# A spectral layer and a mixture of experts on one core: two row groups per gating step, early row fetches tied to their own scatters, zeros in the row memory, a fixed prologue, and a new written order

## The chip, the cores and the metric

The program runs on one NeuronCore of a Trainium2 chip. The metric is the device time of one execution in microseconds. Engines are named as the profile names them: PE is the matmul engine and PEld its weight loads, DVE the vector engine, ACT the scalar engine, POOL the GpSimd engine, and SP the engine that only issues DMAs (SPq, ACTq and POOLq are the instruction queues).

## The reference

The input x has 8 batches of 1856 rows of 256 values. The first half is a spectral layer, the second a mixture of 16 experts in which each row goes to exactly one.

```python
X = np.fft.rfft(x, axis=1);  Xr, Xi = X.real, X.imag
Yr = Xr @ w_r - Xi @ w_i + b_r
Yi = Xr @ w_i + Xi @ w_r + b_i
Yr, Yi = soft_threshold(Yr, 0.01), soft_threshold(Yi, 0.01)
y = np.fft.irfft(Yr + 1j * Yi, n=1856, axis=1).reshape(14848, 256)

g = argmax(y @ w_group)                 # one of 4 groups, and its softmax weight
e = argmax(y @ w_expert[g])             # one of 4 experts of that group, and its weight
out[row] = weight_g * weight_e * (relu(y @ w1[g, e]) @ w2[g, e])
```

## The kernel before

Both Fourier transforms are matmuls with constant matrices. The batches go through in four pairs. For a pair, `first_a` (L342) and `turn_a` (L372) do the first transform stage over eight chunks of x. Fifteen frequency blocks follow: `f_mm` (L668) is the second stage, `f_high`, `f_im`, `f_low`, `f_sum`, `s_high` and `s_low` split its result into high and low parts, `m_both` and `m_each` (L723) multiply by the mixing weights, and `m_re`, `m_relu` and `m_min` (L733, L745, L752, L754) add the bias and apply the threshold. When all fifteen blocks are done, `b_mm` and `b_turn` (L771, L780), then `p_mm` and `p_out` (L790, L801, L803) transform back. The rows of a pair then lie in `vs[pr]`, one half of the tile `vv`; pairs 0 and 2 use the first half, pairs 1 and 3 the second. The second half also serves as the landing place of pair 1's x at the start.

A pair's rows come in eight groups. For each group `p_turn` (L812) turns the rows, `p_copies` (L816) copies them to the tile `yt`, `g_mm` (L831) computes the gate logits and `g_turn` (L841) turns them back. After four groups `route_g` chooses the experts of half a pair, in 32 small steps, most of them on DVE; the 31st (L280) writes `sloti`, the row's place in the list of its expert. Then each of the 16 row sets of that half is sent by one indirect DMA on POOL (`scatter`, L293) to `xs_d`, the lists in HBM: eight halves, 128 scatters. `FLY = (2, 2, 2, 4)` says how many scatters of a pair may be under way: a scatter waits until the one `FLY` before it has landed. Before that, `clear_steps` fills the first 1152 places of each list with zeros, 16 DMAs of 1170 KB from the ACT queue (L436).

For experts 0 to 3 the first 512 rows of each list are computed early, as eight jobs of 256 rows, in between the work of the spectral half: `e_fetch` (L472 and L477, DMAs on SP), `e_ids`, `e_turn` (L481), `e_high` (L892), `e_low` (L896), then `up_mm` (L907) and `down_mm` (L928, L929) with their followers, and `down_out`, a store by an indirect DMA on POOL (L578). Rows 0 to 255 of a list come from pairs 0 and 1, that is from scatters 1 to 64, rows 256 to 511 from pair 2, scatters 65 to 96. The early jobs alternate: expert 0 first half, expert 0 second half, expert 1 first half, and so on. The tiles of the early jobs lie in pools that are opened when the last `m_min` of the last pair is in the list, in the memory of the pools `cf` and `wf` that close there.

The order of PE, ACT and DVE in this first part is written out by hand: the string `ORDER` has one letter per step, and a letter calls the next step of its kind. POOL is not bound to the list. SP's queue is in list order too, but not the prologue's. After the list the remaining rows of all experts are computed by a loop over `JOBS` (L520, L592, L593 and their followers) until the end.

The letters used in the text: e `f_mm`, f `f_high`, g `f_im`, h `f_low`, i `f_sum`, t `s_high`, u `s_low`, j `m_bias`, k `m_both`, q `m_re`, p `m_each`, o `m_min`, c `a_mm`, r `b_mm`, s `b_turn`, y the copy to `yt`, G `g_mm`, H `g_turn`, R a step of routing, S a scatter, Z a clear, F `e_fetch`, T `e_turn`, X `e_high`, Y `e_low`, U `up_mm`, A and B its followers, I `e_ids`, D `down_mm`, K an early store, l a load on SP.

Of the kernel before, what the change touches and what calls it, by code (L numbers as in the profile page):

```python
# [10 lines left out]
F32 = mybir.dt.float32  # L11
# [10 lines left out]
K1 = 15  # L22
# [43 lines left out]
ejefgfhitgeukhijqeptukmoqfgmhicotupjmkfoqmoghepijtefguhkmimqootcjpukdqmfZgmoehiptojfZguemkhcqmoiotjpfZukgdqehi  # L66
mmoptojfZugcmmdkhqoeitopujkmfZgomqheitpclojufZgdmkehoqmitojpfZgukmmedqhplitfZgouojmmchocioktjeqpumfZgddokmqhci
otpjumedfZogmkqehitojpukmoqefZmogpjhitemmukofZogjhrqpitsumekmsfZrgohioqstjusepfZkqgmohripmfZssmotoeghriusjekts
mocjcqdupfZkdcqmgvdompcwlohjmifmtducexdgkohyqcivdopwGHlmcvemfjtoguwhiotkxquypjefkmdomgchvoiqtduGpjwxmkmfgqhyix
ltpoHGeoHjmumkoyfgoqhivtGpHRjeuwRRfkRmglqRxeomhioRpvtjfyRukmRRRqRgehmRRiptGRRomoRHfomujRvegRokhwRqxiRjtuwRpRfk  # L70
gRmxqRmhioopytjRuGmmyRHkqefoopgRhiemtjumGfkooRqgrhjiptuekRHfmegsRsmohiRrSqotussjpkmfmqvogowjpxheityukrqfGmgRom
phsHesmfoRitjouRgrkhieqstRmepsSmSoucRRjSSRvkwRdSRfcgSRxqRhmpyivdSocRtofgGuhRwcSmdljRRiHRdRRkqxomyecSStcRpRRoRd
dRufGljvghcwkHiRxmmqoRpeSytdojRRfScgRmvuhoRmwkqeiRtdlupojfGHSvRkqxmmwRRogpeyoShmSxiGtomvSufghjHRRkiqoteRRRSSRy
pjSuRkvRRmfqGoghwSpmioRteRjuRkRSSHfmxqoSpRghmRoyeRiRSwGtSmjvfwSSRRRRRuSgHkRqhiRxRtmoxRSoRpSyjeuRRkGRfqghimomyp
mmeoRHotoGHuRRfRjSghitrkujeqsRRspRmfkgomRqhrRopssmeSjRfiotRgumrhRitkSReqloRpSusRjfkesmgRRmoqhriotRSjRpuRmSskfW
gqoSmshReiWpmSfvSRgoSvRhtSeuRimjRokqVRSwxowRStuSjpRRkySGmRqmSxRHVfRpgRheyoiWoSSvvWGStVmSSfgjuwokShqwxipmoyeHjm
GtfxgSSmoyHhuekioRGWqHjRRRvwRtpRmRfvRRgRxuwRRShRkWRomqieotSpjukRmfmRRReRgyqVWhRipRSSfoRoxvgRhGmtjmiuRtkuSRRyoq
pRSoRSSWRjRRRVHRwSSekSmfxvghieotmqGoVwHyjpmVVfSxughoGimyotSHGuSSSHljRkkRRSqRRqpRSRSRRRmpmomSRRmoSRoRoRRRRRRFrR
ssRTXRrRYRsSURARRsRUSRRBrUASSABsUSsrSIABBsSDDESsvvSSwwSDWWxJRVvwDSxyGyESvxHGyVSwvHwvxwGWHyvGSWSwSxSHRRSRxyGRRR
# [1314 lines left out]
```

## Time and profile before

| | |
|---|---|
| median of 3 runs | 1055.45 us (1054.57 to 1057.11) |
| the profiled execution | 1054.6 us, span 1052.8 us |
| PE busy | 1016.0 us, 97% of the span |
| DVE, ACT, POOL busy | 704.4, 549.6, 255.1 us |
| mean granted PE clock | 0.993 of 2.4 GHz |
| first part (the written order) | about 0 to 466 us |

The span runs from the first to the last instruction. PE is busy almost throughout, so what counts is where it is not, and where its clock is granted at half. An engine that is idle elsewhere costs nothing unless PE or the chain of rows waits for it. A row of the timeline gives start, duration, engine, line, operation and, in brackets, the idle time before it with what ended it.

### The profile page before, as it was taken

How to read it: one execution, taken by the hardware profiler on the slowest of the kernel's cores; microseconds unless marked ns; L12 is line 12 of the kernel's file. 1: busy time of each engine (PE TensorE's matmuls, PEld its weight loads, DVE VectorE, ACT ScalarE, POOL GpSimd, SP SyncE). 2: the span in 40 equal slices, each digit the busy share in tenths (PEclk: the TensorE clock that was granted, in tenths of full speed). 3: DMA queues.
4: the chain of work that ended last, by engine and by line, in shares of the span. 5: the costliest groups of instructions: out<-in, count | busy, mean ns of one | idle time of the engine just before them, and what ended most of it. 6: DMA issues, size and time to landing. Idle time of an engine off the chain costs nothing.

```text
span 1052.8 us, 20013 instructions
## 1 busy us (share of the span) xinstructions
PE 1016.0 (97%) x7078; PEld 857.9 (81%) x7078; DVE 704.4 (67%) x1764; ACT 549.6 (52%) x1428; POOL 255.1 (24%) x262
## 2 busy tenths in 40 slices
PE   7999999999996999999999999999999999999996
PEld 4886787677874678998899999988889899999995
DVE  6889678988987477647677656475465566566551
ACT  2664685575873464434554535455354455455442
POOL 1000003245355517641121211212211121212111
PEclk9999999999998999999999999999999999999998
DMA  9776401421132156565343232431431431432100
GB/s 379 289 308 239 162 1 38 158 87 69 51 103 81 65 140 185 171 204 148 113 138 112 59 109 53 145 115 49 136 111 51 138 107 52 146 113 63 33 26 25
DMA packets 110065, 125.62 MB, mean 119 GB/s; under 512 B 86250, under 2 KB 86923, under 8 KB 105098
## 3 DMA queue, kind: packets, MB, share of 16 engines
q1 hardware_dynamic: 91386, 74.31, 24.1%
q0 software_dynamic: 11888, 30.67, 7.8%
q10 hardware_dynamic: 6688, 19.34, 4.7%
q8 instruction: 57, 0.93, 0.4%
q14 instruction: 46, 0.38, 0.1%
HBM read 74.32 MB, written 51.75 MB: 120 GB/s over the span
## 4 chain that ended last, share of the span: by engine, by line
PE 79%; issue 6%; DVE 5%; DMA 4%; ACT 3%; POOL 2%; SPq 1%; POOLq 0%; ACTq 0%; DVEq 0%
PE ph L520 26%; PE py L592 16%; PE pw L723 11%; PE py L593 8%; PE pg L668 4%; PE ph L907 3%; DMA xs_d<-v,sloti 2%; PE bank L771 2%; PE bank L342 2%; PE bank L790 2%; PE bank L812 1%; PE py L611 1%; POOL xs_d L293 1%; PE pg L831 1%; PE pg L928 1%
## 5 line engine op out<-in xcount | busy, mean ns | idle before, releaser
L592 PE MATMUL py<-big,hh 128*128 128x512 f32 (+2 forms) x792 | 275.9, 393 | 0.1
L520 PE MATMUL ph<-xth,big 128*128 128x384 f32 (+14 forms) x1024 | 274.3, 346 | 1.6 <-DVE hl L528 0.8
L578 POOL DMA_INDIRECT out_dram<-yo,si x120 | 122.3, 1019 | 484.8 <-DVE si L315 234.0
L528 DVE SCALAR_TENSOR_TENSOR hl<-ph,hh 128x256 fp32r<-128x256 f32 x472 | 157.5, 372 | 98.4 <-ACT hh L524 71.6
L593 PE MATMUL py<-big,hl 128*128 128x256 f32 (+2 forms) x792 | 221.0, 279 | 0.0
L524 ACT ACTIVATE hh<-ph 128x256 fp32r<-128x256 f32 x472 | 140.2, 345 | 113.3 <-PE ph L520 112.6
L520 PEld LDWEIGHTS ph<-xth,big 128*128 128x128 f32 x1024 | 185.4, 188 | 13.6 <-ACT xth L506 1.9
L293 POOL DMA_INDIRECT xs_d<-v,sloti x128 | 126.2, 986 | 284.0 <-DVE big L754 147.8
L520 PE MATMUL ph<-xtl,big 128*128 128x384 f32 (+14 forms) x512 | 176.8, 345 | 1.2 <-DVE xtl L507 1.2
L592 PEld LDWEIGHTS py<-big,hh 128*128 128x128 f32 (+2 forms) x792 | 147.4, 186 | 34.6 <-issue 1.2
L593 PEld LDWEIGHTS py<-big,hl 128*128 128x128 f32 (+2 forms) x792 | 148.0, 187 | 0.3
L600 DVE SCALAR_TENSOR_TENSOR yo<-py,si,yo 128x256 f32<-128x256 f32 (+2 forms) x99 | 47.7, 482 | 108.9 <-ACT yo L599 108.9
L599 ACT ACTIVATE yo<-py,si 128x256 f32<-128x256 f32 (+2 forms) x99 | 46.8, 473 | 131.4 <-PE py L593 121.4
L520 PEld LDWEIGHTS ph<-xtl,big 128*128 128x128 f32 x512 | 96.3, 188 | 7.0 <-DVE xtl L507 2.3
L723 PE MATMUL pw<-wh,xh 128*128 128x256 f32 x360 | 81.3, 308 | 1.6 <-DVE pw L733 1.1
L745 ACT ACTIVATE th<-pw,CF 128x256 f32<-128x256 f32 x120 | 61.1, 526 | 36.8 <-PE pw L723 23.5
L723 PEld LDWEIGHTS pw<-wh,xh 128*128 128x128 f32 x360 | 54.3, 189 | 29.0 <-DVE pw L733 9.4
L723 PE MATMUL pw<-wh,xl 128*128 128x256 f32 x360 | 71.4, 280 | 0.9 <-DVE xl L707 0.9
L723 PE MATMUL pw<-wl,xh 128*128 128x256 f32 x360 | 71.0, 279 | 0.0
L668 PEld LDWEIGHTS pg<-CF,big 128*128 128x128 f32 x480 | 58.4, 191 | 12.6 <-issue 3.1
L668 PE MATMUL pg<-CF,big 128*128 128x128 f32 x480 | 64.6, 278 | 4.2 <-DVE xs L698 2.1
L723 PEld LDWEIGHTS pw<-wh,xl 128*128 128x128 f32 x360 | 54.9, 189 | 1.1 <-DVE xl L707 1.1
(187 smaller groups left out, 1557.4 us busy)
## 6 DMA issues: line engine op xcount, KB each, us to landing
xt<-in_w_dram SPq DMA_DIRECT2D x22, 1024.0 KB, 6.1
xs_d<-zero ACTq DMA_DIRECT2D x16, 1170.0 KB, 5.0
whole<-in_w_dram SPq DMA_DIRECT2D x16, 1024.0 KB, 8.1
xt<-in_x_dram SPq DMA_DIRECT2D x8, 1024.0 KB, 5.4
xg<-xs_d SPq DMA_DIRECT2D x48, 96.0 KB, 2.3
big<-in_x_dram SPq DMA_DIRECT2D x8, 512.0 KB, 4.9
v<-in_x_dram SPq DMA_DIRECT2D x4, 1024.0 KB, 14.1
xg<-xs_d SPq DMA_DIRECT2D x24, 128.0 KB, 3.2
```

The lines of the kernel that those rows point to most:

```text
L293: ins = nc.gpsimd.indirect_dma_start(out=xs_d, out_offset=bass.IndirectOffsetOnAxis(ap=sl_, axis=0), in_=row, in_offset=None, bounds_check ...
L520: nc.tensor.matmul(o[:, :w], lhsT=a_[:, ch, fs], rhs=b_[:, ch, 0:w], start=k == 0, stop=k == 5)
L524: nc.scalar.activation(out=hh[:, f, :m], in_=ov, func=AF.Relu)
L528: nc.vector.scalar_tensor_tensor(out=hl[:, f, :m], in0=ov, scalar=0.0, in1=hh[:, f, :m].bitcast(F32), op0=ALU.max, op1=ALU.subtract)
L578: ins = nc.gpsimd.indirect_dma_start(out=out, out_offset=bass.IndirectOffsetOnAxis(ap=ids.si[0:m, t:t + 1], axis=0), in_=ysb, in_offset=No ...
L592: nc.tensor.matmul(o, lhsT=hh[:, f, ts], rhs=w2b[:, :, f, :], start=f == 0, stop=f == 7, skip_group_check=True)
L593: nc.tensor.matmul(o[:, 0:D], lhsT=hl[:, f, ts], rhs=w2h[:, f, :], start=False, stop=f == 7, skip_group_check=True)
L599: nc.scalar.activation(out=ysb, in_=o[:, D:], func=AF.Copy, scale=gate_w)
L600: nc.vector.scalar_tensor_tensor(out=ysb, in0=o[:, 0:D], scalar=gate_w, in1=ysb, op0=ALU.mult, op1=ALU.add)
L668: nc.tensor.matmul(f_view(pr, k)[:, ch, :, bt], lhsT=zys[pr][:, k, bt, ch * 128:(ch + 1) * 128], rhs=T_v[:, k, :], start=True, stop=True)
L723: nc.tensor.matmul(y[:, half * D:(half + 1) * D], lhsT=a_[:, ch, t], rhs=w_[:, t, ch], start=False, stop=True, skip_group_check=True)
L745: nc.scalar.activation(out=units["t", pr, k][:, ri], in_=psum["m", pr, k][:, ri * D:(ri + 1) * D], func=AF.Relu, bias=nlam, scale=sg_col(0 ...
```

## The change

- `g_mm` and `g_turn` take two row groups per step. The matmuls of two groups (16 of 128 columns in both cases) go to one PSUM tile, and one transpose of 256 columns replaces two of 128. `yt` has two buffers in place of one.
- An early fetch no longer depends on scatters after the 64th (first half) or 96th (second half); it waits for the last `FLY` scatters up to that one. The pools of the early jobs are opened with waits tile by tile, and a tile of 512 bytes is put ahead of the fetched rows.
- `zero` is no tile of its own; it is the first three rows of `vs[0]`, which `b_turn` of pair 0 overwrites.
- The prologue (loads, first transform stage, weights) is in a written order on PE, ACT, DVE and SP. The mixing weights `wri` are loaded behind the second chunk of x; their sums and differences are made on POOL. The last chunk of x is loaded, multiplied and turned in two halves. The constants come in three pieces; `K` is still behind all of them and ahead of pair 1's x.
- `f_low` and `f_sum` may come in either order.
- The string `ORDER` is another one. Counting letters: the first `e_fetch` stands behind 72 scatters (76 before) and is followed at once by its `e_turn` (before: five steps later). The 16 clears stand at places 1 to 245 (72 to 340 before); the first `b_turn` at 287 (275 before). The slot step of pair 1's second half stands behind 54 `m_re` (52 before); the last one, of pair 3, behind 21 `up_mm` and 17 `down_mm` (22 and 17 before), with 5 early stores between it and the last scatter (3 before).

The beginning of the list, and the stretch from the last `m_min` of pair 3 to the slot step of pair 2's second half, before and after:

```
before  ejefgfhitgeukhijqeptukmoqfgmhicotupjmkfoqmoghepijtefguhkmimqootcjpukdqmfZ
after   eZjfgZieftheuhgkijqetugiZpmofkqmcZohtpujkmgqfoihmetpgoZudejkmifocmtqgopjh
before  oRRRRRRFrRssRTXRrRYRsSURARRsRUSRR
after   oFTSrSSRXRRRYRsURURSIAsSlBRARrURARRssrRR
```

The diff, without the string and cut to its core:

```diff
+    one, three = CF1 - (K1 - 1) * 128, CF1 - (K1 - 3) * 128
+    ms.enter_context(tc.manual_schedule(engines=engines))
+    queue.enter_context(tc.manual_schedule(engines={mybir.EngineType.SP}))
+    for c in range(8):
+        if c == 2:
+            nc.sync.dma_start(out=wraw[:, 0:2].rearrange("p a c e -> p (a c e)"), in_=wri)
+        if c == 7:
+            nc.sync.dma_start(out=CF[:, 0:one], in_=cst[:, 0:one])
+            for h in (0, 512):
+                nc.sync.dma_start(out=flat[0][:, c, h:h + 512], in_=flat[1][:, c, h:h + 512])
+        else:
+            nc.sync.dma_start(out=flat[0][:, c], in_=flat[1][:, c])
+    nc.sync.dma_start(out=bias.rearrange("p a e -> p (a e)"), in_=bri)
+    nc.sync.dma_start(out=CF[:, one:three], in_=cst[:, one:three])
+    nc.sync.dma_start(out=craw, in_=cst[:, CF1:CI0])
+    nc.sync.dma_start(out=CF[:, three:], in_=cst[:, three:CF1])
+    nc.sync.dma_start(out=K, in_=cst[:, CK0:CK1])
+    for c in range(0, 8, 2):
+        nc.sync.dma_start(out=xbig[1][:, c:c + 2], in_=x_v[1, :, c:c + 2])
...
+    def last_half(h):
+        o = bank()
+        x = flat[0][:, 7, 512 * h:512 * h + 512]
+        for rows in range(2):
+            for cols in range(2):
+                nc.tensor.matmul(o[64 * cols:64 * cols + 64, 512 * rows:512 * rows + 256], lhsT=cA[64 * rows:64 * rows + 64, 0:64],
+                                 rhs=x[64 * rows:64 * rows + 64, 256 * cols:256 * cols + 256], start=True, stop=True)
...
+    nc.scalar.copy(out=wh[:, 2], in_=w_r)
+    nc.gpsimd.tensor_tensor(out=dif, in0=w_i, in1=w_r, op=ALU.subtract)
+    nc.scalar.copy(out=wh[:, 0], in_=dif)
+    nc.gpsimd.tensor_tensor(out=tot, in0=w_i, in1=w_r, op=ALU.add)
+    nc.scalar.copy(out=whs, in_=tot)
+    nc.scalar.activation(out=wh[:, 1], in_=tot, func=AF.Copy, scale=-1.0)
...
-    zero = cf.tile([128, 3, RW], F32, name="zero")
+    zero = vv[:, 0, 0:3]
...
-        yts[pr, u] = wi.tile([128, 2, 4, 128], F32, name="yt", bufs=1)
+        yts[pr, u] = wi.tile([128, 2, 4, 128], F32, name="yt", bufs=2)
...
-    @steps_of(pairs, u8)
+    @steps_of(pairs, range(0, 8, 2))
     def g_mm(pr, u):
+        o = psum["g", pr, u][:, 0:256].rearrange("p (h v z) -> p v h z", h=2, v=2)
+        for v in range(2):
+            yt = yts.pop((pr, u + v)).rearrange("p c (h x) t -> p c h x t", h=2)
...
         for ins in reads:
             tc.add_to_no_dep_group("early rows", ins.ins)
+            for k in range(64 + 32 * j, len(sent)):
+                tc.declare_no_dep(ins.ins, group=f"row{k + 1}", reason="later rows go to slots behind those of the early jobs")
+            for k in range(64 + 32 * j - FLY[1 + j], 64 + 32 * j):
+                tc.add_manual_dep(ins.ins, sent[k], landed, reason="the early job's rows have landed")
...
-                early["mp"] = ph.enter_context(tc.tile_pool(name="mp", bufs=1))
+                early["mp"] = ph.enter_context(tc.tile_pool(name="mp", bufs=1, reuse_waits="tile"))
...
+                early["mp"].tile([128, 128], F32, name="behind", bufs=1)
```

## Rows read from the trace of the kernel before

**Rows 1.** Windows: length, busy us (and count) of PE, PEld, DVE, ACT, POOL; clock, DMA share, GB/s.

```profile
15.00:25.00 10.00, 6.07 (x50) 4.99 (x43) 7.85 (x12) 5.04 (x12) 3.77 (x3) 1.00 1.03 421
105.00:300.00 195.00, 191.39 (x1804) 146.53 (x1804) 159.47 (x388) 133.27 (x311) 57.91 (x59) 1.00 0.23 81
300.00:329.20 29.20, 24.82 (x252) 20.79 (x250) 25.66 (x73) 20.70 (x47) 14.54 (x15) 1.00 0.29 99
329.20:340.20 11.00, 6.25 (x36) 1.61 (x28) 6.13 (x14) 0.62 (x1) 6.12 (x7) 0.72 0.36 102
340.20:380.20 40.00, 36.93 (x333) 24.13 (x333) 20.10 (x42) 20.00 (x40) 17.14 (x18) 0.95 0.25 68
```

**Rows 2.** Waits of SP's queue, 280 to 460 us: total us, times, longest.

```profile
SPq L472 <- DMA xs_d<-v,sloti: 75.8, 8, 36.9
SPq L472 <- DVE big L754: 24.2, 1, 24.2
```

**Rows 3.** Timeline around the first early fetch, 328 to 346 us.

```profile
328.68 0.47 DVE L754 SCALAR_TENSOR_TENSOR big<-pw,CF,th 128x256 f32<-128x256 f32 x1
...
333.70 0.38 SPq L472 DMA_DIRECT2D xi<-xs_d  x1
...
338.01 0.71 DVE L481 STREAM_TRANSPOSE sl<-xg 128x512 f32<-128x512 f32 x1 [4.46 <-DMA xg<-xs_d]
...
344.92 0.23 DVE L280 TENSOR_SCALAR sloti<-slot,K 128x16 int32<-128x16 f32 x1
```

**Rows 4.** Timeline: scatters 49, 64, 81 and 96, the second early fetch.

```profile
283.36 0.97 POOL L293 DMA_INDIRECT xs_d<-v,sloti  x1 [10.36 <-ACT big L862]
...
306.09 0.97 POOL L293 DMA_INDIRECT xs_d<-v,sloti  x1 [0.30 <-issue]
...
345.93 0.97 POOL L293 DMA_INDIRECT xs_d<-v,sloti  x1 [7.78 <-DVE hl L917]
...
370.59 0.97 POOL L293 DMA_INDIRECT xs_d<-v,sloti  x1 [0.40 <-DMA xs_d<-v,sloti]
...
372.99 0.39 SPq L472 DMA_DIRECT2D xi<-xs_d  x1
...
380.18 0.39 PE L907 MATMUL ph<-xtl,big 128*128 128x256 f32 x1 [0.22 <-DVE xtl L896]
```

**Rows 5.** Timeline: the loop's first fetch and one of its first matmuls.

```profile
456.61 0.38 SPq L472 DMA_DIRECT2D xi<-xs_d  x1
...
466.07 0.45 PE L520 MATMUL ph<-xtl,big 128*128 128x400 f32 x1 [0.31 <-DVE xtl L507]
```

**Rows 6.** Timeline of DVE: the 54th `m_re`.

```profile
294.55 0.49 DVE L733 SCALAR_TENSOR_TENSOR pw<-pw,CF,bias 128x256 f32<-128x256 f32 x1 [0.24 <-PE pw L723]
```

**Rows 7.** Groups of instructions by line, first part: busy us, mean ns, idle before.

```profile
L831 PE MATMUL pg<-yt,wg 128*32 128x128 f32 x512 | 20.6, 279 | 4.3 <-ACT yt L816 3.1 <-DVE L L841 0.8 <-DVE xs L698 0.5
L841 DVE STREAM_TRANSPOSE L<-pg 128x128 f32<-128x128 f32 x32 | 9.8, 307 | 14.9 <-PE pg L831 14.8
```

**Rows 8.** Timeline of DVE: the first `b_turn`.

```profile
82.35 1.25 DVE L780 STREAM_TRANSPOSE v<-bank 128x1024 f32<-128x1024 f32 x1 [0.38 <-PE bank L771]
```

**Rows 9.** Timeline of the prologue, 15 to 19 us.

```profile
15.09 0.62 ACT L408 CAST wh<-xt 128x512 fp32r<-128x512 f32 x1 [12.61 <-DMA xt<-in_wri_dram]
...
15.79 1.27 POOL L409 TENSOR_TENSOR wl<-xt,wh 128x512 fp32r<-128x512 f32 x1 [14.31 <-ACT wh L408]
...
17.01 1.16 PE L668 MATMUL pg<-CF,big 128*128 128x128 f32 x8 [1.48 <-DVE big L372]
...
18.87 0.69 DVE L693 TENSOR_TENSOR xl<-pg,xh 128x512 fp32r<-128x512 f32 x1 [0.32 <-ACT xim L685]
```

**Rows 10.** DMA queues, 100 to 108 us: packets, MB, share of 16 engines' time.

```profile
q1 hardware_dynamic: 272, 1.05, 38.9%
q10 hardware_dynamic: 388, 1.18, 37.0%
```

**Rows 11.** Chain of waits: one `up_mm` at full clock (start, us, matmuls).

```profile
388.42 1.42 PE ph L907 x12
```

More of the change, by code (lines that the diff above doesn't have):

```diff
@@ L377, in drain @@
             pass
[L379 removed]
+    warm = pg.tile([128, 512], F32, name="pg")
     for _ in range(14):
[L381 removed]
+        nc.tensor.matmul(warm[:, 0:256], lhsT=ones, rhs=smask[16], start=True, stop=True)
     for _ in range(2):
@@ L387, in spectral_moe @@
+    for i in range(7):
         o = bank()
         first_a(0, i, o)
-        a_last = turn_a(0, i, o)
-    craw = wf.tile([128, 2 * D], F32, name="th")[:, 0:128]
-    wraw = xp.tile([128, 4, 2, D], F32, name="xt")
-    nc.sync.dma_start(out=wraw[:, 0:2].rearrange("p a c e -> p (a c e)"), in_=wri)
-    nc.sync.dma_start(out=craw, in_=cst[:, CF1:CI0])
-    bias = cf.tile([128, 2, D], F32, name="bias")
-    nc.sync.dma_start(out=bias.rearrange("p a e -> p (a e)"), in_=bri)
-    nc.sync.dma_start(out=CF[:, first:], in_=cst[:, first:CF1])
@@ L411, in spectral_moe @@
-    mix_parts(2, 0)
-    nc.scalar.copy(out=sl, in_=craw)
-    nc.vector.tensor_tensor(out=bias[:, 0], in0=bias[:, 0], in1=bias[:, 1], op=ALU.subtract)
-    behind.close()
-    nc.vector.memset(nlam, -2 * LAM)
+        turn_a(0, i, o)
+        if i == 1:
+            for _ in range(8):
+                nc.tensor.matmul(warm[:, 0:256], lhsT=ones, rhs=smask[16], start=True, stop=True)
+    for h in range(2):
+        last_half(h)
     T_v = CF[:, CF1 - K1 * 128:CF1].rearrange("p (k m) -> p k m", m=128)
-    late = ExitStack()
@@ L427, in spectral_moe @@
     nc.sync.dma_start(out=wgp, in_=wgate)
-    late.close()
-    zero = cf.tile([128, 3, RW], F32, name="zero")
+    zero = vv[:, 0, 0:3]
     nc.gpsimd.memset(zero, 0.0)
+    cf.tile([128, 16], F32, name="behind")
     def clear_steps():
@@ L621, in spectral_moe @@
     jobs = EJOBS
-    engines = {mybir.EngineType.PE, mybir.EngineType.Activation, mybir.EngineType.DVE}
     sgo = _OFF["SG"][0]
@@ L685, in f_im, with f_read @@
         nc.scalar.copy(out=xi, in_=f_part(pr, k)[:, :, 1])
-        if pr == k == 0:
-            mix_parts(0, 2)
-            mix_parts(1, 3)
+        if (pr, k) == (0, 0):
+            nc.vector.tensor_tensor(out=bias[:, 0], in0=bias[:, 0], in1=bias[:, 1], op=ALU.subtract)
+        if (pr, k) == (0, 1):
+            nc.scalar.copy(out=sl, in_=craw)
+    read = set()
+    def f_read(pr, k):
+        if (pr, k) in read:
+            del psum["f", pr, k]
+        read.add((pr, k))
     @steps_of(pairs, k15)
```

112 lines of the change are left out of this document (50 added, 62 removed).

## The prediction

> **What bounds the kernel now.** I read the windows first. PE is the engine that counts, and the change reaches only the first part. PE stands idle there for 3.9 us between 15 and 25, for 3.6 us between 105 and 300, and for 12.2 us between 300 and 380 (4.4, 4.8 and 3.1) [rows 1]. In the worst piece, 329.2 to 340.2, the clock is also granted at 0.72 on average, part of it at the lower of the two levels.
>
> The waits of SP say why. A fetch of early rows (L472) waits for scatters eight times, 75.8 us in all, and once 24.2 us for the last `m_min` (L754) [rows 2]. The timeline shows the first: the last `m_min` starts at 328.68, the fetch is issued at 333.70, DVE stands 4.46 us before `e_turn` until the rows are there at 338.01, and behind `e_turn` DVE holds back the routing and PE [rows 3]. Then a second chain sets the pace. The slot step of pair 2's second half (344.92) releases sixteen scatters on POOL, 345.93 to 370.59, 1.64 us each; the fetch for the second early job goes at 372.99, and PE starts on it at 380.18 [rows 3, 4]. That is 35.3 us from slot step to matmul, 9.6 of them behind the last scatter's start. At the end of the first part the same happens once more: behind the last scatters the loop's first fetch goes at 456.61, and a matmul at 466.07 waits for the rows' low part [rows 5].
>
> **The change, part by part.** All times are of the profiled execution: span 1052.8 us, 1054.6 us in all, 0.85 below the median of the three runs; differences are carried over to that median.
>
> *The first early fetch.* It needs scatter 64. In the list before, 76 scatters stand ahead of it and it waits for all of them. Now it waits for two that started by 306.09 [rows 4], and, with memory released tile by tile and 512 bytes put ahead, probably for the last second-stage matmul in place of the last `m_min`. Then the rows lie ready and `e_turn` starts right behind the last `m_min`. Between that and the slot step DVE has about the same work: four `b_turn`, `e_turn` and `e_low` in both, 14 routing steps for 17, and an id step (two operations) and one low half more. So the 4.46 us of waiting go; 0.5 us I keep back for waits that it covered: -4.0 us. Bounds: 0, if the fetch stays late; -5.5, if the slow clock behind it goes too (about 3 us of 128x256 matmuls at half speed cost up to 1.5).
>
> *What is late next: POOL.* The scatters of pair 2 cannot go faster than two at a time. In the list after, the slot step of pair 1's second half stands behind 54 `m_re`, which puts it near 294.55 [rows 6], where the first of its scatters started at 283.36 before [rows 4]. POOL then has 48 scatters in a row. Spacing: 1.52 us for scatters 49 to 64, 1.64 for 81 to 96 [rows 4]; 47 spacings at 1.5 are 70.5 us. With the next item's 1.5 us the first starts near 293.9 and the last at 364.4, while the path over pair 2's own slot step gives 370.59 - 1.5 - 4.0 = 365.1. The two meet; I add 1.0 us for their interference. Bounds: 0 at 1.45 us a scatter, +6 at 1.64.
>
> *Two groups a step, two `yt` buffers.* The matmuls are the same 16 per pair of groups. DVE saves a transpose in two: 32 of 307 ns [rows 7] become 16 of 256 columns; from 307 ns for 128 columns and 1.25 us for 1024 [rows 8] one takes about 440, so 2.8 us less on an engine that is 82% busy in 105 to 300 [rows 1]. PE waited 3.1 us for `yt` in all [rows 7]. Part of the 3.6 us of idle time goes: I take -1.5 for this and the new list up to pair 3, with -3.6 (all) and +3.6 (as much new) as ends. What pays is the logits: a pair of groups is turned back only when both are done, which is one reason why the slot steps move back.
>
> *The prologue.* The first second-stage matmul stays at 17.0: it waits 1.5 us for DVE's turns of the eight chunks [rows 9], and two half turns (0.71 us for 512 columns [rows 3]) are no shorter than a whole one (1.25). Behind it the weights were late: `wri` landed at 15.09, as the last of 4.9 MB (sizes here and below from the shapes in the code). Now 1.6 MB stand up to it, 3.4 MB less, 8.0 us at 421 GB/s [rows 1], so 7.1 us; the sums on POOL (two of 1.27) and two copies of 0.62 [rows 9] end near 10.9. That would give back up to 2.4 us, the idle time of 15 to 25 less that wait. But the first clear now stands second in the list. ACT issues it near 11 us, in the midst of the loads, and DVE's part of that step copies from `K`, which lies behind 6.15 MB: 1.2 MB or 2.9 us after 15.09, 18.0 without the clear. With its 1.33 MB beside it, half of the engines' time each as when a load and a clear ran together [rows 10], `K` comes up to 3.2 us later, 21.2, and `f_low` (18.87 before [rows 9]) is queued on DVE behind that copy; the mixing waits for it. -2.4 and +2.4: I take 0, ends -2.4 and +3.0 (pair 1's x late as well).
>
> *The zeros.* `b_turn` of pair 0 now waits until all clears have read the zeros, with DVE's thresholds and splits queued behind it and PE's mixing behind those. Until then 12.6 MB of loads and 19.3 MB of clears go through: 75.7 us at 421 GB/s, from about 3 us on, some 80 with the landing; the first `b_turn` came at 82.35 [rows 8]. So nothing, if the queues never run dry, and a prologue that is faster by over 2 us would give it back here. 0, ends 0 and +4.
>
> The measured 421 GB/s is where the Trainium skill speaks against the change. DMA: Bandwidth & Descriptors, section Specifications, gives one core about 358 GB/s of HBM; by that estimate the clears would be down near 92 us, and `b_turn` would stand nearly 10. The trace does not bear it out (421 over ten whole microseconds), so it stays inside the rival on the clears.
>
> *The end of the first part.* The last slot step stands one `up_mm` earlier, 1.4 us [rows 11], but one or two more early stores share POOL with the last scatters, 1.27 us each (0.97 and 0.30 of issue [rows 4]), 1.9: +0.5. What follows is PE work without idle time to speak of and is passed on whole.
>
> Sum: 0 + 0 - 1.5 - 4.0 + 1.0 + 0.5 = -4.0 us: 1050.6 in the profile, 1051.4 as a median.
>
> **The rivals.**
> 1. *POOL becomes the bound* (slower). For it: 48 scatters without a pause, two in flight, from a slot step that moved back by about 11 us. At 1.64 us each from 295.4 (nothing gained before) the last starts at 372.5 and PE has the rows at 382.1, 1.9 late; at the end +0.5, and PE, out of work for longer, restarts at half clock, another 0.6: +3.0, 1058.5. It decides from a spacing of 1.6 on. Against: a scatter that waits for no landing takes 1.27 us (0.97 and 0.30 [rows 4]), so the spacing can fall as well as rise.
> 2. *The clears collide* with the loads and with `b_turn`: +3.0 and +1.5 (a late front makes the zeros less late), against -4.0 elsewhere: 1056.0. For it: the first two clears fall inside a stretch in which the engines are full [rows 1]. Against: 2 us of room before `b_turn`.
> 3. *The early fetch is not early*, as its memory is still held by the last `m_min` (the 24.2 us of [rows 2]): issued at 329.3, rows 4.3 us later, and `e_turn` stands first behind the last `m_min`, so DVE waits as long as before. -4.0 is lost: 1055.4.
> 4. *More is won*: all of 3.6, 4.0, and scatters at 1.4, midway between 1.27 and 1.52 (16 times 0.24 = 3.8 us), less 2 for what comes next: -9.4, 1046.0.
>
> **How the numbers follow.** Forecast 0.47 (its own range 1048 to 1054.5), POOL 0.13, clears 0.12, no early fetch 0.08, more 0.20. 0.2% is 2.1 us, about what a measurement of this kernel tells from no change. Faster (below 1053.3): 0.43 of the forecast, 0.20 of the last, 0.01 of the others, 0.64. Slower (above 1057.6): 0.12 of POOL, 0.04 of the clears, 0.16. The rest, 0.20, is no change. A tenth lies below 1045 and a tenth above 1058.
>
> **What would show it.** The fetch issued before the last `m_min`, and `e_turn` without a wait behind it; PE idle in that piece under 2 us and the clock whole. The wait for the second early job should remain, the only one above 3 us. POOL's pauses between scatters 49 and 96 should be gone. `f_low` no earlier than 18, waiting for `K`; the first `b_turn` near 82. I am wrong if that piece is unchanged, if scatter 96 starts after 370, or if DVE stands at the first `b_turn` for more than 2 us.

## The result, and the profile after

The changed kernel takes 1066.7 us (median of 4, 1065.55 to 1066.99) where the one before takes 1056.1 (median of 4): ratio 1.0096, 95% interval 1.0076 to 1.0116. It is slower by 10.6 us; the forecast was 4 us faster. The profiled execution takes 1066.98 us, span 1065.2, mean granted clock 0.982.

The windows of the kernel after, with the columns of [rows 1]; the second and the last are stretches that [rows 1] doesn't have:

```profile
15.00:25.00 10.00, 6.23 (x46) 4.54 (x46) 5.15 (x10) 2.67 (x7) 0.00 (x0) 0.94 1.03 391
25.00:50.00 25.00, 22.91 (x156) 19.90 (x155) 14.13 (x32) 13.27 (x33) 0.00 (x0) 0.82 0.99 395
105.00:300.00 195.00, 190.96 (x1806) 146.90 (x1799) 159.01 (x364) 129.12 (x300) 47.29 (x48) 1.00 0.22 74
329.20:340.20 11.00, 7.19 (x66) 4.50 (x62) 7.68 (x26) 4.33 (x10) 7.04 (x8) 0.89 0.28 86
340.20:380.20 40.00, 34.47 (x286) 22.60 (x287) 20.66 (x37) 16.26 (x33) 20.30 (x22) 0.86 0.36 119
380.20:400.00 19.80, 9.81 (x89) 7.32 (x88) 6.95 (x20) 6.54 (x14) 5.86 (x6) 0.74 0.52 137
```

The kernel before in these two stretches:

```profile
25.00:50.00 25.00, 24.48 (x198) 20.24 (x197) 19.59 (x42) 17.09 (x40) 0.00 (x0) 1.00 0.72 285
380.20:400.00 19.80, 19.80 (x172) 18.23 (x173) 16.52 (x43) 11.83 (x22) 4.11 (x4) 1.00 0.46 148
```

105 to 300 is as it was. New are a slow start (25 to 50 at a clock of 0.82, where it was 1.00) and 380 to 400, in which PE works half of the time; in the kernel before it was busy there for all of 19.8 us. To see where time is lost, I take for some steps their start less the matmul time that stands ahead of them in the list (each step's matmuls at full clock, as [rows 11] has it for `up_mm`). What remains is everything that was not PE work at full speed. A low half is here the step B, which follows `up_mm`:

```
start less PE work ahead of it, us      before   after   difference
third m_re                               20.7     28.3    +7.6
first b_turn                             22.2     31.1    +8.9
last b_turn of pair 2                    38.8     44.6    +5.8
last m_re of pair 3                      46.0     52.2    +6.2
first low half, first early job          57.3     63.4    +6.1
first low half, second early job         63.6     81.8   +18.2
last low half of the first part          69.6     80.4   +10.8
(span                                  1052.8   1065.2   +12.4)
```

So 8.9 us are lost at the start, 2.7 won from there to the end of the spectral half, nothing won at the first early job, 12.1 lost up to the second, of which 7.4 come back by the end of the part; 1.6 more are lost behind it, for which no run gives a cause. A single row is good to some 2 or 3 us, as neighbouring steps stand in another order (over the `b_turn`s of pair 1 the difference lies between 7 and 12). Each has its rows.

*The start.* ACT's timeline of the kernel after; lines of ACTq are DMA issues, L449 is a clear, L766 `m_relu`:

```profile
14.88 0.36 ACTq L447 DMA_DIRECT2D xs_d<-v  x1
15.94 0.68 ACTq L449 DMA_DIRECT2D xs_d<-v  x1
...
21.94 0.54 ACTq L449 DMA_DIRECT2D xs_d<-v  x1
22.52 0.59 ACT L692 CAST xh<-pg 128x512 fp32r<-128x512 f32 x1 [2.86 <-PE pg L680]
...
31.91 0.54 ACTq L449 DMA_DIRECT2D xs_d<-v  x1
32.50 0.48 ACT L766 ACTIVATE th<-pw,CF 128x256 f32<-128x256 f32 x1 [6.40 <-DMA v<-in_x_dram]
```

ACT stands twice. The cast at 22.52 needs matmuls that had ended at 19.66; the profile names a later one of that line, but what ACT's queue waits for is the clear at 21.94. The second time it is the clear at 31.91; DVE's first `m_min` waits the same 6.39 us for ACT, and the first `b_turn` comes at 92.86 (82.35 before [rows 8]). What the clears waited for: in the trace each DMA names the semaphore that it counts up and waits on. The DMAs of SP and ACT take eight of them in turn, so an issue waits until the transfer eight issues back has landed, and on ACT everything queued behind it waits too:

```
issue on ACT        its semaphore was last used by     landed    issued
short clear         pair 0's x, last half chunk         14.85     14.88
second clear        the short clear                     21.92     21.94
third clear         pair 1's x, third load of four      31.89     31.91
```

*The first early fetch.* The waits of SP's queue, 280 to 480 us (total us, times, longest), as in [rows 2]:

```profile
SPq L485 <- DVE big L775: 111.2, 1, 111.2
SPq L485 <- DMA xs_d<-v,sloti: 48.1, 5, 29.9
```

DVE's timeline, as in [rows 3]:

```profile
336.79 0.47 DVE L775 SCALAR_TENSOR_TENSOR big<-pw,CF,th 128x256 f32<-128x256 f32 x1
343.53 0.71 DVE L494 STREAM_TRANSPOSE sl<-xg 128x512 f32<-128x512 f32 x1 [6.27 <-DMA xg<-xs_d]
...
356.41 0.23 DVE L279 TENSOR_SCALAR sloti<-slot,K 128x16 int32<-128x16 f32 x1
```

The fetch still waits for the last `m_min` (L775) and is issued at 337.40. `e_turn` now stands right behind that `m_min`, so DVE waits 6.27 us where it waited 4.46 [rows 3], and the slot step comes 19.6 us behind the last `m_min` (16.2 before).

*POOL.* POOL's timeline: scatters 49, 64, 74, 81, 83 and 96, as in [rows 4]:

```profile
302.51 0.97 POOL L292 DMA_INDIRECT xs_d<-v,sloti  x1 [18.30 <-DVE xl L713]
...
326.62 1.23 POOL L292 DMA_INDIRECT xs_d<-v,sloti  x1 [0.30 <-DMA xs_d<-v,sloti]
...
346.00 0.97 POOL L292 DMA_INDIRECT xs_d<-v,sloti  x1 [3.71 <-DMA xs_d<-v,sloti]
...
357.97 0.97 POOL L292 DMA_INDIRECT xs_d<-v,sloti  x1 [0.94 <-DVE big L890]
...
364.54 0.97 POOL L292 DMA_INDIRECT xs_d<-v,sloti  x1 [4.32 <-ACT big L885]
...
387.01 0.97 POOL L292 DMA_INDIRECT xs_d<-v,sloti  x1 [0.30 <-issue]
```

PE's first matmul on the second early job's rows:

```profile
395.21 0.58 PE L934 MATMUL ph<-xth,big 128*128 128x256 f32 x1 [9.47 <-ACT xth L919]
```

48 scatters stand in a row, 84.5 us for 47 spacings, 1.80 each. Up to 64 they take 1.61. The long pauses follow two loads of early weights (1 MB each, issued at 339.82 and 357.90): 4.68 and 2.85 us from one scatter to the next behind the first, 5.30 and 3.31 behind the second. Scatter 96 starts at 387.01 (370.59 before [rows 4]) and PE stands 9.5 us.

*Gating.* The two groups of the first part that answer to [rows 7]:

```profile
L854 PE MATMUL pg<-yt,wg 128*32 128x128 f32 x512 | 17.5, 276 | 1.5 <-ACT yt L837 0.7 <-DVE xs L719 0.6
L864 DVE STREAM_TRANSPOSE L<-pg 128x256 f32<-128x256 f32 x16 | 6.9, 434 | 15.7 <-PE pg L854 15.7
```

### The profile page after: what moved, and what is told of

Same layout as the page of the kernel before. It is cut to its first block, busy times and chain, and to the rows that moved or that the text cites. A ratio compares the mean times of both kernels' runs of the same rounds, so it can differ in the third digit from the quotient of the medians.

```text
span 1065.2 us, 20038 instructions
## 1 busy us (share of the span) xinstructions
PE 1018.3 (96%) x7094; PEld 865.4 (81%) x7094; DVE 698.3 (66%) x1747; ACT 549.4 (52%) x1429; POOL 259.4 (24%) x264
## 4 chain that ended last, share of the span: by engine, by line
PE 58%; issue 2%; DVE 1%; POOL 1%; ACT 1%; DMA 0%; SPq 0%; POOLq 0%; DVEq 0%; ACTq 0%
PE ph L533 25%; PE py L605 15%; PE py L606 8%; PE ph L934 4%; PE pg L955 2%; PE py L624 1%; PE pg L956 1%; POOL out_dram L591 1%; DVE xtl L520 0%; ACT xth L519 0%; DVE x L494 0%; DMA xs_d<-v,sloti 0%; DMA xg<-xs_d 0%; DVE hl L541 0%; ACT yo L612 0%
## 5 line engine op out<-in xcount | busy, mean ns | idle before, releaser
L292 POOL DMA_INDIRECT xs_d<-v,sloti x128 | 128.6, 1005 | 311.7 <-DVE big L775 189.1
L612 ACT ACTIVATE yo<-py,si 128x256 f32<-128x256 f32 (+2 forms) x99 | 46.9, 474 | 131.5 <-PE py L606 121.4
L766 ACT ACTIVATE th<-pw,CF 128x256 f32<-128x256 f32 x120 | 60.4, 524 | 47.9 <-PE pw L744 23.0
L934 PE MATMUL ph<-xth,big 128*128 128x256 f32 x256 | 53.6, 298 | 14.8 <-ACT xth L919 14.8
```

The source lines that it names most:

```text
L292: ins = nc.gpsimd.indirect_dma_start(out=xs_d, out_offset=bass.IndirectOffsetOnAxis(ap=sl_, axis=0), in_=row, in_offset=None, bounds_check ...
L766: nc.scalar.activation(out=units["t", pr, k][:, ri], in_=psum["m", pr, k][:, ri * D:(ri + 1) * D], func=AF.Relu, bias=nlam, scale=sg_col(0 ...
L934: nc.tensor.matmul(o[:, i * 256:(i + 1) * 256], lhsT=a_[:, ch, fs], rhs=b_[:, ch, :], start=k == 0, stop=k == 5)
```

## The experiments

They ran on five other chips (A to E), on which every kernel was slower (the kernel before 1090 to 1101 us, the changed one 1096 and 1100); so times are ratios to the kernel before on the same chip, and steps are compared with the changed kernel's own profile where it ran beside them (B and D). Of the changed kernel's 28 us on one of them, 27.9 are lost by the end of the first part (its last low half at 500.4 for 472.5, the span 1093.2 for 1065.2). Stops that no visible step ends stand there. This is one of DVE (total us, times, longest), of a kind that the two profiles of the first chip don't have and all 18 runs below do:

```profile
DVE L L864 <- remote: 12.5, 1, 12.5
```

| run | ratio to before, 95% interval | first `m_relu` | first `b_turn` | from last `m_min` to slot step, to scatter 96 |
|---|---|---|---|---|
| after_again (chip B) | 1.0078 (1.0041 to 1.0115) | 32.2 | 92.4 | 18.3, 48.0 |
| late_clears_2 (B) | 1.0011 (0.9978 to 1.0045) | 24.8 | 86.0 | 18.6, 49.0 |
| all3 (B) | 0.9966 (0.9934 to 0.9998) | 25.2 | 85.5 | 11.1, 38.4 |
| before_pairs (B) | 1.0203 (1.0149 to 1.0257) | 26.7 | 92.9 | 14.8, 39.8 |
| late_clears (A) | 0.9881 (0.9829 to 0.9933) | 25.0 | 85.7 | 19.3, 49.4 |
| own_sg (A) | 0.9941 (0.9909 to 0.9973) | 31.7 | 90.8 | 11.0, 44.1 |
| l1112 (A) | 0.9962 (0.9929 to 0.9996) | 32.1 | 90.8 | 17.2, 43.7 |
| before_early_clears (A) | 1.0086 (1.0044 to 1.0127) | 38.3 | 94.5 | 16.3, 40.2 |
| late_sg (C) | 0.9966 (0.9932 to 1.0000) | 25.4 | 86.5 | 11.1, 44.4 |
| late_l (C) | 1.0002 (0.9971 to 1.0032) | 25.2 | 85.6 | 17.3, 43.0 |
| late_singles (C) | 1.0074 (1.0034 to 1.0114) | 24.8 | 85.9 | 18.7, 48.5 |
| all3_fly (C) | 1.0158 (1.0099 to 1.0217) | 24.9 | 85.4 | 12.0, 34.1 |
| after_3 (D) | 1.0003 (0.9970 to 1.0037) | 32.4 | 91.2 | 18.0, 48.0 |
| own_sg_2 (D) | 0.9985 (0.9953 to 1.0016) | 32.5 | 91.5 | 11.0, 44.5 |
| late_sg_2 (D) | 0.9921 (0.9890 to 0.9952) | 25.5 | 85.9 | 11.2, 45.1 |
| pool_clears (D) | 1.0122 (1.0080 to 1.0164) | 42.6 | 101.6 | 18.5, 46.9 |
| sp_clears (E) | 0.9953 (0.9922 to 0.9985) | 24.9 | 86.4 | 18.9, 49.0 |
| two_clears (E) | 0.9987 (0.9956 to 1.0017) | 30.3 | 89.1 | 18.4, 48.4 |

The ratio of one kernel moves from chip to chip: the changed kernel has 1.0096, 1.0078 and 1.0003, the one with late clears 0.9881 and 1.0011. So only ratios of one chip are evidence; where ratios of two chips are set beside each other, the text says so.

**The changed kernel again**, as a reference.

> The changed kernel itself, once more, beside the others of this group, since the chip of the first group was slower with every kernel (the kernel before took 1101 us on it). Theory: its ratio to the kernel before is 1.008 to 1.012, as at first, and the first m_relu comes near 32.5 us, the first early fetch near 337, scatter 96 near 387. Rival (the first ratio belonged to that one chip): within 0.4% of the kernel before.

> The changed kernel itself, as the reference on one chip for the three kernels beside it. Expected: a ratio to the kernel before of 1.007 to 1.010, first m_relu near 32, 18 to 20 us from the last m_min to the slot step of pair 2's second half, 48 to 50 us to scatter 96.

The loss came again on chip B (1.0078), but not on D, where 1.007 to 1.010 was expected and 1.0003 measured: there the changed kernel is no slower than the one before. The first `m_relu` comes as at first (32.2 and 32.4), scatter 96 later (394.4 and 399.4 for 387.0). What the expectations call the third `m_re`, at 33 (26.8 in the kernel before), is the second.

**The start.** late_clears and late_clears_2 are one kernel: five letters Z of the changed list are moved.

```diff
-eZjfgZieftheuhgkijqetugiZpmofkqmcZohtpujkmgqfoihmetpgoZudejkmifocmtqgopjhmuki...
+ejfgieftheuhgkijqetugipmofkqmcohtpujkmgqfoihmetpgoudeZjkmifocmZtqgopjhmZukiqf...
```

> The changed kernel, with its first five clears of the list (places 1 to 54) moved behind the first 58 to 94 letters. Theory (a clear is issued from ACT's queue; its issue waits until the transfer issued eight before it has landed, so the third clear, at 31.9 us, holds ACT until pair 1's x is there, and the stop of 6.4 us there goes over to DVE and PE): the first m_relu comes near 26 instead of 32.5, the third m_re near 27 instead of 33, the first b_turn near 86 instead of 92.9, and the kernel is 5 to 7 us faster than the changed one, 1060 to 1062, a ratio to the kernel before of about 1.004. Rival (the new order of the loads, and weights made on POOL, cost the 7 us whatever the clears do): the first m_relu stays at or after 31, within 1.5 us of 1066.7. Second rival (the time is won at the start and lost at the first b_turn, which waits for the last clear to have read the zeros): first m_relu near 26, but the first b_turn still after 91, and no more than 2 us gained in all.

> The changed kernel with its first five clears moved behind the first 58 to 94 letters, once more, for a comparison with the changed kernel on one chip. Theory (the early clears' issues, which wait for transfers and hold ACT, cost the start): first m_relu near 25, first b_turn near 86, and 6 to 9 us faster than the changed kernel, a ratio to the kernel before of 1.001 to 1.004. Rival (the start is won and lost again behind POOL's 48 scatters): scatter 96 still after 384 and no more than 3 us gained.

ACT's timeline in late_clears_2, the first `m_relu`:

```profile
24.82 0.47 ACT L766 ACTIVATE th<-pw,CF 128x256 f32<-128x256 f32 x1 [1.94 <-PE pw L744]
```

Its window 25 to 50:

```profile
25.00:50.00 25.00, 25.00 (x205) 20.91 (x203) 19.47 (x44) 17.11 (x42) 0.00 (x0) 1.00 1.03 396
```

PE is busy for all of the 25 us at full clock. The first `b_turn` comes 6.4 us earlier than in the changed kernel on that chip, the ratio falls by 0.0067, 7.3 us. own_sg_2 and late_sg_2 below, which differ by the same five letters on chip D, say the same: 0.0064, 7.0 us. The theory holds, and the second rival in part: `b_turn` starts at 85.96, 0.27 us behind the landing of the last clear (85.69), after 2.06 us of waiting on DVE. The rival of late_clears_2, that POOL's scatters eat the gain, fails in the time, though scatter 96 comes after 384 as it said (49.0 us behind the last `m_min`, 48.0 in the changed kernel).

Stop or traffic? Four kernels bear on it. before_early_clears is the kernel before with its first five Z at places 1 to 50. pool_clears issues the changed kernel's first five from POOL, sp_clears (with the short one) from SP's queue; two_clears moves only the third to fifth.

```diff
-            nc.scalar.dma_start(out=xs_d[e * CAP:e * CAP + NZ]...
+            (nc.sync if e < 5 else nc.scalar).dma_start(out=xs_d[e * CAP:e * CAP + NZ]...
```

> The kernel before, with its first five clears moved to the places that they have in the changed kernel's list (behind the first 1, 4, 22, 30 and 50 letters); the zeros stay in a tile of their own. Theory (issue of the clears stops ACT): ACT stands some 5 us at the third clear until pair 1's x has landed, the third m_re comes near 32 instead of 26.8, and the kernel takes 3 to 7 us more than before, 1059 to 1063: part can be won back by idle time that the list had later. Rival (only with the zeros in the rows' memory, whose tile also receives pair 1's x, does a clear wait for that x): the first m_relu stays near 26 and the time within 2 us of before.

> The changed kernel, with the first five clears issued from POOL's queue in place of ACT's, at the same places of the list. The transfers run beside the loads as before; what their issue waits for holds POOL, which has nothing else to do before 180 us. Theory (the stop of ACT at a clear's issue costs the start): first m_relu at 25 to 28, third m_re at 29 to 32, first b_turn near 86 to 88, 5 to 7 us faster than the changed kernel beside it. Rival (the clears' traffic beside the loads of x costs it): first m_relu still after 30, within 2 us of the changed kernel. Between them (both): 28 to 30, 3 us.

> The changed kernel with its first five clears (and the short one ahead of them) issued from SP's queue, behind the loads that stand there and ahead of those of pair 2's x; ACT issues the other eleven. The clears' traffic still runs beside the loads of pair 1's x from about 18 us on, but their issues no longer hold ACT. Theory (the stop of ACT is the price): first m_relu at 25 to 28, third m_re at 29 to 32, first b_turn at 85 to 88. Rival (the traffic is the price, as pair 1's x comes late): first m_relu at 30 or later. The time itself follows: 5 to 7 us below the changed kernel in the first case, within 2 us in the second, with the uncertainty that it isn't timed beside it on this chip.

> The changed kernel with the first two clears where they are (places 1 and 5) and the next three moved behind the first 74 to 94 letters. Theory (each stop is its own price: about 2 us at the second clear, about 6 at the third): ACT stands 2 to 3 us at the second clear, the first m_relu comes at 27 to 29 instead of 32.5 (25 with all five moved), the third m_re at 31 to 33. Rival (the first two clears' traffic delays what follows as much as the stops do): first m_relu at 30 or later.

Two of them changed the traffic more than was meant. In before_early_clears ACT is free so early that the first clear goes out at 1.91 us, ahead of most loads of x; in pool_clears nothing holds POOL, and all five go out from 1.79 on. `K` lands at 22.0 and 35.1 us in place of 18.3, and the first `m_relu` comes at 38.3 and 42.6: neither expectation fits, and clears ahead of the loads are shown to cost. sp_clears is the clean one. SP's queue there:

```profile
18.45 13.10 SPq L449 DMA_DIRECT2D xs_d<-v  x5
31.67 4.74 SPq L656 DMA_DIRECT2D xt<-in_x_dram  x2
```

ACT's first `m_relu` there:

```profile
24.92 0.47 ACT L766 ACTIVATE th<-pw,CF 128x256 f32<-128x256 f32 x1 [1.97 <-PE pw L744]
```

The same five clears run between 18.5 and 49.5 us, the DMA engines are full (1.03 of the window 25 to 50), and the first `m_relu` is at 24.92, as with late clears. So full queues alone cost nothing here: the price is paid where ACT stops. But sp_clears has its clears behind pair 1's x, and the traffic set how long the stop was. The third load of that x, for which ACT stands, landed at 31.89 in the changed kernel and at 31.66 in two_clears, where two clears go out among these loads; without a clear among them it landed at 26.80 (sp_clears) and 26.89 (late_clears_2). With that landing the stop of 6.4 us would have been about 1.4 (an estimate from these landings). In two_clears ACT stops only at the second clear; its timeline:

```profile
22.66 0.59 ACT L692 CAST xh<-pg 128x512 fp32r<-128x512 f32 x1 [3.24 <-DMA xs_d<-v]
...
30.27 0.48 ACT L766 ACTIVATE th<-pw,CF 128x256 f32<-128x256 f32 x1 [4.03 <-PE pw L744]
```

`m_relu` at 30.3 is what the rival said (30 or later). Its reason, traffic that costs as much as the stops, is not what the rows show: `K` lands at 18.2 as in sp_clears, ACT stands 3.24 us for the short clear, not 2, and behind that PE runs at a granted 0.92 and 0.90 in 15 to 25 and 25 to 50 (1.00 in sp_clears), so the next matmuls are late as well.

**The early fetch.** own_sg and own_sg_2 are one kernel; late_sg and late_sg_2 have the late clears too.

```diff
+    sgt = cf.tile([128, 48], F32, name="sgt")
+    nlam = sgt[:, 47:48]
...
+    nc.gpsimd.tensor_copy(out=sgt[:, 0:3 * K1], in_=CF[:, 0:3 * K1])
...
-        return CF[:, sgo + i * K1 + k:sgo + i * K1 + k + 1]
+        return sgt[:, sgo + i * K1 + k:sgo + i * K1 + k + 1]
```

> The changed kernel, with the 45 sign columns and the constant that the second stage's last steps read copied to a tile of their own, so that the tile CF, over which the early rows are fetched, is read for the last time by the last f_mm and not by the last m_min. Theory (memory is released by whole tiles, and the first early fetch waits for the last reader of CF): the fetch is issued near 328 to 331 instead of 337.4, its rows are there before e_turn, DVE's wait of 6.3 us before e_turn falls below 1 us, and the slot step of pair 2's second half comes 5 to 6 us earlier than 356.4. Since scatters of pair 2 then still run without a pause up to 387, the time of the kernel falls by 0 to 2 us only. Rival (that wait is what costs): it falls by 4 to 6 us. Second rival (something else holds the fetch, such as the scatters' own landing): it is still issued after 336.

> The changed kernel with the sign columns in a tile of their own, its early clears where they are. Theory (the held fetch costs 4 to 5 us by itself, and the start costs 7 independently of it): ratio 0.003 to 0.005 below that of the changed kernel beside it, 11 us from the last m_min to the slot step, 44 us to scatter 96. Rival (the gain appears only when the start is early, as POOL is the bound otherwise): within 0.002 of it.

> The changed kernel with the late clears and the sign columns in a tile of their own, the weight loads where they were. Theory (the early fetch was held by the tile, and its gain is mostly eaten by the scatters behind it): the first early fetch is issued before the last m_min, e_turn starts within 1 us of it, the slot step of pair 2's second half comes 10 to 12 us behind the last m_min instead of 19, scatter 96 about 44 us behind it instead of 49, ratio 0.997 to 1.000 to the kernel before (late clears alone 1.001). Rival (the scatters eat all of it): scatter 96 still 48 us or more behind the last m_min, ratio 1.001.

> The changed kernel with late clears and the sign columns in a tile of their own, beside the changed kernel on one chip. Theory (the two effects add): ratio 0.010 to 0.013 below the changed kernel's, 0.996 to 0.998 to the kernel before. Rival (they overlap): 0.008 below or less, at or above 1.000.

SP's queue in late_sg_2, the first early fetch:

```profile
336.17 0.38 SPq L488 DMA_DIRECT2D xi<-xs_d  x1
```

DVE there, the last `m_min`, `e_turn` and the slot step:

```profile
346.09 0.48 DVE L778 SCALAR_TENSOR_TENSOR big<-pw,sgt,th 128x256 f32<-128x256 f32 x1
346.48 0.70 DVE L497 STREAM_TRANSPOSE sl<-xg 128x512 f32<-128x512 f32 x1
...
357.30 0.23 DVE L279 TENSOR_SCALAR sloti<-slot,K 128x16 int32<-128x16 f32 x1
```

The fetch goes 9.9 us ahead of the last `m_min`, `e_turn` follows it without a wait, and the slot step comes 11.2 us behind it. What SP's queue waits for there is the second stage's matmuls, in place of the last `m_min`: the cause of the held fetch is shown. But scatter 81 starts 8.9 us behind that slot step (366.2), because the scatters ahead of it are still running; of 7 us won at the slot step some 3 arrive at scatter 96. In the time: own_sg_2 is 0.0018 below after_3, inside the intervals and as its rival said (within 0.002); late_sg_2 is 0.0082 below, 9 us, nearer to its rival's 0.008 than to the theory's 0.010. How much of that is the fetch's own is not settled: 2 us by own_sg_2, 1.7 when the 7.3 us that the clears cost on chip B are taken off the 9, 5 by late_sg (C) beside late_clears_2 (B).

**The weight loads.** l1112 moves two letters l, one into POOL's pause and one behind the second fetch, with the four splits that this takes; late_l has the late clears too, and all3 all three edits.

> The changed kernel with two loads of early weights (1 MB each) moved out of the stretch in which POOL has 48 scatters in a row: one ahead of it, into POOL's pause near 295 us (with three of the splits that free its buffer), one behind the second early fetch (with the split that reads it). Theory (a weight load beside the scatters delays their landing: 4.7 and 2.9 us between two scatters behind the first load, 5.3 and 3.3 behind the second, 1.6 elsewhere): scatter 96 starts 6 to 10 us earlier than 387.0, 377 to 381, PE starts on the second early job's rows near 386 to 390 instead of 395, and the kernel is 4 to 8 us faster than the changed one. Rival (the gaps come from POOL's other work or from the fetch of early rows): scatter 96 stays after 385 and the time within 1.5 us.

> The changed kernel with the late clears and the two weight loads moved, the fetch as in the changed kernel. Theory (with the loads away, scatters 65 to 96 take 1.6 us each, but the slot step of pair 2's second half, late by the fetch, now sets scatter 81): scatter 81 within 2 us behind that slot step, 96 some 25 us later, 44 to 45 us behind the last m_min, ratio 0.998 to 1.001. Rival (loads don't matter): spacing 65 to 96 stays at 1.85 or more.

> The changed kernel with the late clears, the sign columns in a tile of their own, and the two weight loads moved out of the scatters' way, all at once. Theory (the three causes are start, early fetch and scatters, and the rest of the change is worth 1 to 4 us): scatter 96 near 369, DVE's wait before the first e_turn below 1 us, PE on the second early job's rows near 378, and the kernel 2 to 6 us faster than the one before, 1050 to 1054 where that one takes 1056. Rival (what is left behind the three, above all the routing's later slot steps, still costs): no faster than the kernel before, 1056 to 1060.

POOL's timeline in l1112, scatters 65 and 80:

```profile
336.79 0.97 POOL L292 DMA_INDIRECT xs_d<-v,sloti  x1 [3.09 <-ACT th L766]
...
359.64 0.97 POOL L292 DMA_INDIRECT xs_d<-v,sloti  x1 [0.30 <-issue]
```

1.52 us each, 1.64 in late_l and 1.66 in all3; in the twelve runs of the changed list that leave the loads where they were, 1.77 (own_sg) to 2.05 (own_sg_2): the loads do stretch the scatters. The rival's fetch of early rows goes at 349.53 in l1112, in the midst of them, and from there to scatter 80 no spacing is over 1.99. The times of scatter 96 that I wrote (377 to 381, 369) were missed, as all steps come later on these chips; counted from the last `m_min` it comes 5 to 6 us earlier. That this is worth time of its own is not shown: all3 and late_sg have the same ratio, late_l is 0.0009 below late_clears_2, each on two chips.

all3_fly lets four scatters of pair 2 be on their way:

```diff
-FLY = (2, 2, 2, 4)
+FLY = (2, 2, 4, 4)
```

> The changed kernel with all three edits (late clears, sign columns in a tile of their own, two weight loads moved), and four scatters of pair 2 on their way at a time instead of two. Theory (POOL's scatters set the pace up to the second early job, and every second one waits for a landing): scatters 65 to 96 stand 1.30 to 1.45 us apart instead of 1.58 to 1.66, scatter 96 starts 15 to 20 us behind the slot step of pair 2's second half (27 with the three edits alone, 26 in the kernel before), and the kernel is 2 to 5 us faster than with the three edits alone, a ratio to the kernel before of 0.992 to 0.995. Rival (the work for the rows is no longer what PE waits for there): scatter 96 earlier by as much, but the ratio stays at 0.996 to 0.998.

Both expectations failed. Scatters 65 to 80 start 1.28 us apart, as hoped, but from scatter 70 on DVE starts nothing for 16.3 us, and PE's matmuls come singly up to 351.9 and then not at all up to 359.8. DVE's timeline in all3_fly:

```profile
341.87 0.18 DVE L283 TENSOR_TENSOR base<-base,inc 128x16 f32<-128x16 f32 x1
358.39 0.45 DVE L867 STREAM_TRANSPOSE L<-pg 128x256 f32<-128x256 f32 x1 [16.34 <-remote]
```

PE's there:

```profile
349.17 0.78 PE L747 MATMUL pw<-wh,xl 128*128 128x256 f32 x2 [0.34 <-issue]
351.29 0.59 PE L747 MATMUL pw<-wl,xh 128*128 128x256 f32 x2 [1.33 <-issue]
```

The last `m_min` slips from 345.2 (all3) to 364.3, and the kernel is 0.0192 above late_sg on its own chip, as much as above all3 on another. In all3 DVE has no such stop there, but one of 11.5 us later, beside scatters 85 to 92 (its waits between 300 and 400 us):

```profile
DVE L L867 <- remote: 16.3, 2, 11.5
```

**Gating.** late_singles gates each group in a step of its own again (letters G and H doubled); before_pairs brings pairs, two `yt` and the zeros in the rows' memory into the kernel before, with its clears closer together.

> The changed kernel with the late clears, in which each row group is gated in a step of its own again (with two yt buffers; the first of two groups gated and turned back a few letters ahead of the second). Theory (gating in pairs saves DVE 16 transposes, 2 to 3 us, and PE some short waits in 105 to 300): PE busy in 105 to 300 lower by 0.5 to 2 us than with late clears alone, ratio to the kernel before 1.001 to 1.004. Rival (it is worth nothing, PE's waits for yt went with the second buffer alone): ratio 1.000 to 1.002, and no wait of PE for yt over 1 us in all.

> The kernel before, in which two row groups are gated in a step, with two yt buffers and the zeros in the rows' memory as in the changed kernel; of each two gating letters the second stays in its place. Its clears stand closer together (all sixteen within the first 200 letters, the first where it was), so that they have read the zeros when the first b_turn comes. Theory (the gating in pairs is worth 1 to 3 us: PE's waits for yt of 3.1 us go, and DVE turns half as often): PE busy in 105 to 300 up from 191.4 to 192.5 or more and the kernel 0.5 to 3 us faster than the one before. Rival (the slot steps come later, since a pair of groups is turned back when both are done): scatter 49 after 285 and the kernel 1 to 4 us slower.

late_singles is 0.0073 above late_clears_2 (another chip) and 0.0072 above late_l (its own), more than expected; PE is busy for 183.1 us of 105 to 300, 186.8 in late_l. PE's idle time ahead of `g_mm` grows from 2.3 to 10.8 us, 3.7 of it for `yt`; but the places of the doubled letters were chosen by hand, so this is an upper bound for what pairs are worth. before_pairs tells nothing of gating: its denser clears stop ACT, PE is busy for 38.81 of 60 to 105 (44.61 before), and the first `b_turn` comes at 92.9.

## Why the prediction was wrong

- *The prologue, 0 (-2.4 to +3.0).* This step failed, by 8.9 us, outside both bounds. The weights were early and `K` landed at 18.3, as said for a start without a clear. I priced the clear as traffic ahead of `K`, but it went out at 15.94, behind `K`, which landed at 18.30 without early clears too (late_clears_2). sp_clears shows that the clears' traffic behind the loads costs nothing there. What costs is the issue: it waits on ACT for a transfer eight issues back, one that the clears' own traffic had made 5 us late. The trace of before had it in view, in SP's issues: pair 1's first load goes at 12.01, when the transfer eight back landed at 12.00; I did not ask where that wait would stand in ACT's queue.
- *The first early fetch, -4.0.* Failed: nothing won. The guess "for the last second-stage matmul in place of the last `m_min`" was wrong: the rows lie over CF, the released unit is the tile, and its last reader is the last `m_min`. That is rival 3, given 0.08. The size was about right at the slot step: with the columns in their own tile, it comes 5.0 us nearer to the last `m_min` than before (11.2 for 16.2). In the time of the kernel own_sg_2 shows 2, not clear of noise.
- *POOL, +1.0 (0 to +6).* The place of the first scatter was right once the late start is added (302.5 for 293.9 + 8.9), the spacing was not: 1.80 us for 1.5, beyond the 1.64 of the bound, since both weight loads fall beside the scatters. Scatter 96 starts at 387.0, not 365. It costs 12.1 us at the second early job; 7.4 come back, 6.0 of them because the list before lost 6.0 in the same stretch (63.6 to 69.6 in the table). That leaves 4.7 for this and the end of the part, for which 1.5 stood. What the stretched scatters cost in time is not shown: no kernel is shown to be faster for the moved loads.
- *Gating, -1.5 (-3.6 to +3.6).* The number fits: 2.7 us won between the first `b_turn` and the last `m_re`, waits for `yt` 0.7 us instead of 3.1, a transpose of 434 ns for the 440 estimated. That gating made it is not shown: 2.7 lies within the spread of single rows, and PE stands idle for 4.0 us in 105 to 300, where 3.6 were to shrink. late_singles allows up to 8.
- *The zeros, 0 (0 to +4).* Right here: `b_turn` at 92.86 waits for nothing, the last clear had landed at 91.42. The other half of the sentence is shown too: with a faster start 2 us are given back there (late_clears_2). By the figure of 358 GB/s (the Trainium skill, DMA: Bandwidth & Descriptors, section Specifications) that landing would, as an estimate, have been near 92 even with queues that never ran dry. They moved 417 GB/s in 15 to 25 us of sp_clears, and the last clear of late_clears_2 landed at 85.7, so the traces stay with the measured rate.
- *The rivals.* 1, 2 and 3 each named a place where time was lost, and all three came true at once (2 with another mechanism). They did not exclude each other, yet I gave each a chance and a time of its own, as though the rest of the forecast stood. Added up from their own prices (+3.0 for 1, +4.5 for 2, 0 for 3's fetch, -1.5 for gating) they give +6, on the right side but 4.6 short of the measured 10.6.

With the two causes at start and fetch removed, the changed kernel lies at or below the one before: late_sg 0.9966 and late_sg_2 0.9921. On chips C and D that is 4 and 9 us faster, where 4 were forecast; but on D the changed kernel itself was no slower than the one before, and on the chip of the prediction the kernel without the two causes was not run.

## What to carry to other kernels

A DMA issued from an engine that computes is a wait of that engine: before it is moved forward, list the transfers issued ahead of it, find the one whose semaphore it takes over, and see when that lands with the moved transfer running beside it. When a buffer is to be filled early, ask which tile lies under it and who reads that tile last, in its smallest corner. And where several rivals sit in different places of the program, add their prices instead of choosing among them.

## What the runs showed of the hardware that was not expected

- Engines stop beside scatters. In all3_fly eleven scatters (70 to 80) 1.28 us apart go with 16.3 us in which DVE starts nothing. That it was the missing pause that stopped DVE is not shown: with two in flight DVE or ACT has such stops of 3 to 13 us in each of the 17 other runs on these chips (all3: 11.5 us beside scatters 1.48 us apart), and the two profiles of the first chip have none. The Trainium skill (SBUF — State Buffer, section SBUF: two separate sides) has DVE and GpSimd share one pair of ports that one of them locks for an instruction. DVE's stop could be that. The rows speak against it as the only cause: PE and ACT, which by that page wait for no port, stand too (PE for 0.3 to 1.3 us at a time in that stretch, ACT for 7.8 us at once in after_again), and POOL is busy 0.97 us of each 1.28. Which it is was not tried.
- A load of 1 MB beside scatters of which two are in flight delays single scatters by 1.3 to 3.7 us (2.85 to 5.30 instead of 1.6). Not every long spacing is a load's: the kernel before has 3.26 us ahead of scatter 69 with none under way.
- The same kernel loses 28 us more on another chip, nearly all in the part with scatters, where stops stand that the profile puts down to no step. Why one chip has them and another not stays open.
